# Attention within hash buckets and a mixture-of-experts stage: divisions moved to another engine, one comparison for six, and a new instruction order

## The chip, the cores and the metric

The kernel runs on one core of a Trainium2 chip. The metric is the device time of one execution in microseconds (us); three runs of the kernel before gave 447.36 us as their median (446.34 to 448.22). One further execution was taken with the hardware profiler, and all rows below are from it. A core has a matrix engine (TensorE, "PE" in the profile, its weight loads "PEld"), a vector engine (VectorE, "DVE"), a scalar engine (ScalarE, "ACT"), GpSimd ("POOL") and SyncE ("SP"), which here only issues DMAs.

## The reference

```python
# B, H, S, D = 4, 8, 768, 64; proj has 6 columns
q_bits = (einsum('bhsd,dk->bhsk', q, proj) > 0); k_bits likewise
mask   = bucket(q_bits)[..., :, None] == bucket(k_bits)[..., None, :]
scores = where(mask, q @ k.T / sqrt(D), -1e9)
attn   = exp(scores - scores.max(-1))
attn   = attn / (attn.sum(-1) + 1e-9)
x      = (attn @ v), heads side by side              # (4, 768, 512)
gate   = x @ w_gate                                  # (4, 768)
for b in range(4):                                   # the 128 tokens with the highest gate
    top = argpartition(-gate[b], 128)[:128]
    ye  = relu(x[b, top] @ w1) @ w2                  # 512 -> 1024 -> 512
    out[b, top] = x[b, top] + sigmoid(gate[b, top]) * ye   # other tokens: out = x
```

## The kernel before

There are 32 heads (head 8b+h belongs to batch b). For each head the kernel loads q and k transposed, hashes them (a matmul and a comparison, `signs`), and places the sign bits beside the head's rows as extra rows of one operand, so that one matmul gives scores with the bucket mask already in them. Three stages follow, each cut in units that the order names by short words:

- The row maxima. `mx` units (PE, L559) form bounds from the keys in two halves; `kd`, the difference of the halves, is computed once per head on DVE (L553) or POOL (L550). `re` (ACT, L567) takes the positive part, `rd` (DVE, L575) reduces it with the second matmul to a maximum per row. When all six `rd` of a head are done, `mt` (PE, L584) turns the column of maxima into a row, `mc2` (ACT, L589) copies it out of PSUM and a DMA places it as a further row of the operand.
- The scores. `s` units (PE, L604 and L608, a high and a low part) write PSUM and `e` (ACT, L622 and L624) takes the exponentials P.
- The product with V. P is split in a high half, which is read in place, and the rest R = P - high(P), which is a subtraction on DVE (`r`, L643) or on POOL (`g`, L646). `a` (PE, L668) multiplies both by V into one PSUM tile per head, with the row sums in an extra column. `rc` (DVE, L678 to L680) takes the reciprocals of the sums and `n` (ACT, L692) divides. That PSUM tile has one buffer: the next head's `a.x.0` starts when the divisions of this head are done. Input for the splits comes from `xh` (ACT, L440) and `xl` (DVE, L445), the high and low part of q and k.

After the last head of a batch, `sc` (DVE, L706) forms the gate scores and `choose` (in the order `c0`, `c1`, `c2`; for the last batch `rank_last`) ranks the tokens, marks in `sel` which token goes to which of 128 slots (L799, L1108), turns this by matmuls into indices, and gathers the tokens by an indirect DMA. `e0` to `e3` are the experts: the gathered tokens are transposed by PE (L836) and split by ACT, DVE, ACT (L843, L844, L845: xth, xtl, xtb) before the matmuls with w1 and w2. The experts of batches 0 to 2 run beside the attention of later batches.

Nothing reorders instructions at run time: each engine executes its own in the order in which the code issues them, and semaphores between engines are added where data need them. That order is a hand-written string, `ORDER`, of some 2770 words such as `mx.13.1.0` or `n.0.2`; a second string, `BANKS`, gives the PSUM bank of each `mx` tile. A POOL subtraction is issued so that it waits for the last DVE instruction issued before it that is marked with `mine` (`turn`). A `wu.N` word is filler: N matmuls of constants (L305) whose result nobody reads, put where PE would stand idle at the start.

Of the kernel before, what the change touches and what calls it, by code (L numbers as in the profile page):

```python
# [41 lines left out]
i0 wu.30 ia.0 ia.2 X.0 dd.0.3 wu.23 hx.0.1 X.1 X.2 da.0.0 sx.0.1.0 sx.0.1.1 hx.0.0 sx.0.0.1 da.0.2 sx.0.0.0  # L42
kv.0 X.3 V.0 xh.1 pa.1.0 lc pa.1.1 wu.5 h.0.0.1.2 sg.0.0.1.2 ia.1 h.0.1.1.2 sg.0.1.1.2 ps.1.1 da.0.1 wu.18
mx.0.1.0 ps.1.0 w pb.0.1 mx.0.2.0 xh.0 re.0.1 xl.0 pb.0.2 mx.0.0.0 pb.0.3 re.0.0 wu.2 mx.0.2.1 mx.0.0.1 rd.0.0
mx.0.1.1 rd.0.1 re.0.2 rd.0.2 mx.0.3.0 re.0.3 ia.3 h.0.1.2.4 sg.0.1.2.4 wu.1 mx.0.3.1 mx.0.4.0 re.0.4 ir.1
h.0.0.2.4 rd.0.3 pb.0.0 sg.0.0.2.4 ps.2.1 ir.0 wu.1 mx.0.5.0 vh.0 re.0.5 mx.0.5.1 mx.0.4.1 rd.0.4 rd.0.5
ps.2.0 kd.1 wu.16 mx.1.1.0 mx.1.0.0 xh.2 re.1.1 pa.2.1 mx.1.2.0 re.1.2 mx.1.5.0 re.1.0 vl.0 w wu.2 mx.1.0.1 mc
rt.0 rk.0 mx.1.1.1 pa.2.0 pb.1.0 rd.1.0 mx.1.3.0 rd.1.1 wu.3 mx.1.2.1 rd.1.2 wu.3 mx.1.4.0 re.1.5 re.1.3 wu.3
mx.1.5.1 mx.1.3.1 re.1.4 mx.1.4.1 w xl.1 sv.0 rd.1.3 w s.0.6 pb.1.2 xh.3 s.0.3 s.0.8 rd.1.4 w pb.1.1 e.0.6
s.0.0 e.0.3 s.0.5 e.0.8 ps.3.0 e.0.0 rd.1.5 mt.1 g.0.4 pb.1.3 mc2.1 mr.1 sh.0 pa.3.1 xl.3 s.0.4 kv.2 s.0.2  # L50
mx.2.1.0 mx.2.2.0 sl.0 ps.3.1 e.0.5 e.0.2 re.2.1 mx.2.0.1 V.1 s.0.1 mx.2.0.0 s.0.7 re.2.0 e.0.1 g.0.1 mx.2.2.1
r.0.0 a.0.0 re.2.2 e.0.7 r.0.2 rd.2.0 mx.2.1.1 rd.2.1 rd.2.2 s.1.6 X.6 e.0.4 r.0.3 mx.2.4.1 mx.2.5.0 re.2.5
xl.2 s.1.0 mx.2.3.0 e.1.0 re.2.3 mx.2.4.0 re.2.4 mx.2.3.1 rd.2.3 s.1.3 s.1.2 e.1.2 X.4 rd.2.4 g.0.5 pa.3.0
vh.1 a.0.1 a.0.2 X.5 xh.4 X.7 w e.1.3 a.0.3 pb.2.0 a.0.4 a.0.5 mx.2.5.1 e.1.6 s.1.8 e.1.8 kv.3 mx.3.0.0
mx.3.2.0 re.3.2 r.1.0 mx.3.0.1 rd.2.5 mt.2 s.1.5 e.1.5 mc2.2 re.3.0 g.1.2 rc.0 mr.2 s.1.7 e.1.7 g.1.5 s.1.1
pb.2.1 e.1.1 mx.3.1.0 n.0.0 n.0.1 r.1.4 n.0.2 pb.2.3 vl.1 rd.3.0 h.1.0.0.4 pb.2.2 sg.1.0.0.4 h.1.1.0.4
sg.1.1.0.4 s.1.4 w ps.5.0 mx.3.1.1 ps.4.1 r.1.1 re.3.1 mx.3.2.1 pa.4.0 w w mx.3.4.0 re.3.4 a.1.0 a.1.1 w a.1.2
xh.6 mx.3.5.1 mx.3.3.0 rd.3.1 rd.3.2 e.1.4 r.1.3 mx.3.5.0 re.3.3 re.3.5 pa.4.1 pb.3.2 mx.3.4.1 s.2.0 ps.4.0
xl.4 pb.3.1 s.2.1 mx.3.3.1 e.2.0 e.2.1 s.2.2 rd.3.3 rd.3.4 rd.3.5 w pb.3.3 s.2.5 s.2.3 e.2.2 xh.5 a.1.3 e.2.3
a.1.4 e.2.5 sv.1 sh.1 kd.4 mx.4.0.0 a.1.5 sl.1 re.4.0 mt.3 pa.5.1 mc2.3 mr.3 mx.4.1.0 mx.4.0.1 s.2.4 re.4.1  # L60
pa.5.0 rc.1 n.1.1 ps.5.1 n.1.0 pb.3.0 g.2.0 n.1.2 rd.4.0 mx.4.1.1 V.2 e.2.4 rd.4.1 g.2.1 mx.4.3.0 mx.4.2.0
re.4.2 re.4.3 mx.4.4.1 s.2.6 e.2.6 s.2.8 e.2.8 g.2.2 mx.4.2.1 rd.4.2 a.2.0 s.2.7 mx.4.5.0 ps.6.0 re.4.5 pa.6.1
w g.2.3 xl.5 pb.4.3 mx.4.4.0 a.2.1 pb.4.0 pb.4.2 e.2.7 a.2.2 a.2.3 kv.5 pb.4.1 mx.4.3.1 w w rd.4.3 re.4.4
s.3.3 e.3.3 s.3.4 e.3.4 s.3.5 mx.4.5.1 mx.5.2.0 e.3.5 re.5.2 s.3.0 e.3.0 rd.4.4 rd.4.5 s.3.2 w mt.4 mc2.4
mx.5.0.0 e.3.2 mx.5.1.0 mr.4 re.5.1 re.5.0 s.3.6 e.3.6 mx.5.0.1 X.8 pa.6.0 ps.6.1 mx.5.2.1 r.2.4 a.2.4 g.3.2
g.3.3 r.2.5 a.2.5 rc.2 s.3.7 X.9 vh.2 e.3.7 s.3.1 rd.5.0 e.3.1 s.3.8 e.3.8 mx.5.1.1 mx.5.4.0 mx.5.3.0 s.4.1
pb.5.2 s.4.3 n.2.1 pb.5.3 r.3.0 pb.5.0 g.3.1 rd.5.1 rd.5.2 w r.3.4 pb.5.1 n.2.2 s.4.0 mx.5.3.1 n.2.0 vl.2
mx.5.5.0 a.3.0 a.3.1 a.3.2 re.5.4 re.5.5 e.4.0 e.4.1 kv.6 g.3.5 sv.2 re.5.3 rd.5.3 mx.5.4.1 s.4.2 e.4.3 xh.7
mx.5.5.1 mx.6.5.0 re.6.5 rd.5.4 rd.5.5 xl.7 e.4.2 g.4.1 g.4.0 s.4.4 e.4.4 mx.6.1.0 s.4.5 re.6.1 mt.5 mc2.5
mx.6.0.0 mr.5 e.4.5 s.4.6 xl.6 sh.2 sl.2 V.3 re.6.0 pa.7.1 a.3.3 a.3.4 a.3.5 rc.3 e.4.6 mx.6.2.0 mx.6.0.1  # L70
n.3.1 ps.7.0 X.10 s.4.8 e.4.8 mx.6.1.1 s.4.7 g.4.4 pb.6.3 ps.7.1 rd.6.0 n.3.0 mx.6.2.1 mx.6.3.0 r.4.2 r.4.3
X.11 s.5.0 pb.6.0 rd.6.1 n.3.2 e.4.7 r.4.5 w pa.7.0 re.6.3 w w xh.8 e.5.0 pb.6.1 w s.5.2 re.6.2 a.4.0 a.4.1
a.4.2 a.4.3 a.4.4 a.4.5 rc.4 vh.3 rd.6.2 mx.6.3.1 e.5.2 n.4.0 s.5.6 e.5.6 mx.6.4.1 w g.5.0 s.5.1 mx.6.4.0
re.6.4 rd.6.3 rd.6.4 mx.6.5.1 rd.6.5 s.5.3 h.2.0.0.4 h.2.1.0.4 n.4.2 pb.6.2 e.5.1 s.5.5 mt.6 e.5.3 sg.2.0.0.4
s.5.4 n.4.1 mc2.6 mr.6 pa.8.0 kd.7 mx.7.1.0 s.5.7 e.5.5 s.5.8 mx.7.1.1 vl.3 pb.7.0 e.5.4 e.5.7 mx.7.0.0 e.5.8
r.5.1 re.7.0 g.5.2 a.5.0 pa.8.1 sg.2.1.0.4 a.5.1 a.5.2 r.5.5 ps.8.1 g.5.4 re.7.1 V.4 w w xh.9 mx.7.2.1
# [1103 lines left out]
```

## Time and profile before

| | |
|---|---|
| median of 3 runs (lowest to highest) | 447.36 us (446.34 to 448.22) |
| the profiled execution, its own time | 448.66 us |
| its span, first to last instruction | 446.8 us |
| PE busy | 430.0 us, 96% |
| DVE, ACT, POOL busy | 351.3, 343.5, 219.9 us |
| mean granted TensorE clock | 0.991 of full speed |

The profiled execution takes 1.86 us more than its span, and 1.30 us more than the median of the runs. Busy shares are means over a span whose stages have different limits. PE's own busy time contains its stretches at a lower clock and its overlap of one matmul with the next, so that 96% is no statement that PE runs at its peak. Durations of single instructions are in ns in groups by line and in us in a timeline.

### The profile page before, as it was taken

What the parts mean: (1) busy time and instruction counts of PE and PEld (TensorE: products, weight loads), DVE (VectorE), ACT (ScalarE), POOL (GpSimd) and SP (SyncE); (2) the same over time, 40 slices, a digit from 0 to 9 for tenths busy, and PEclk for the clock granted to TensorE, in tenths of its full rate; (3) what the DMA queues carried; (4) which work ended last, traced back from release to release, by engine and by line L of the source; (5) the groups of instructions that cost most, each with busy time, mean ns of one, the idle gap of its engine ahead of it and who ended that gap; (6) DMA issues with size and microseconds to landing.
All of it is one profiled execution on the core that took longest, in us unless ns stands there. A gap on an engine that the chain in (4) does not pass through costs nothing.

```text
span 446.8 us, 14202 instructions
## 1 busy us (share of the span) xinstructions
PE 430.0 (96%) x5530; PEld 353.0 (79%) x5539; DVE 351.3 (79%) x872; ACT 343.5 (77%) x830; POOL 219.9 (49%) x165
## 2 busy tenths in 40 slices
...
GB/s 253 175 216 201 216 227 222 194 218 180 246 204 181 154 158 221 111 226 198 196 161 154 168 177 194 177 177 193 206 150 155 88 143 56 37 107 25 72 49 23
DMA packets 32802, 72.72 MB, mean 163 GB/s; under 512 B 5024, under 2 KB 11372, under 8 KB 32736
## 3 DMA queue, kind: packets, MB, share of 16 engines
...
## 4 chain that ended last, share of the span: by engine, by line
PE 74%; DVE 9%; DMA 8%; issue 4%; ACT 3%; SPq 1%; POOLq 0%; ACTq 0%; POOL 0%; DVEq 0%
PE av L668 19%; PE mx L559 15%; PE st L604 13%; PE st L608 12%; DMA X<-in_qk_dram 4%; PE mh L868 4%; PE yp L906 3%; PE hp L364 3%; DVE R L643 3%; PE ws L305 2%; DMA A<-mr 2%; DVE me L575 1%; DVE jks L706 1%; DMA A<-XH 1%; PE sp L509 1%
## 5 line engine op out<-in xcount | busy, mean ns | idle before, releaser
L646 POOL TENSOR_TENSOR R<-P 128x768 f16<-128x768 f32 x100 | 158.8, 1598 | 115.8 <-ACT P L624 26.4
L604 PE MATMUL st<-A 97*128 97x512 f32 (+1 forms) x384 | 129.3, 350 | 0.4 <-DMA A<-mr 0.4
L608 PE MATMUL st<-B 128*128 128x512 f32 (+1 forms) x384 | 125.0, 340 | 0.0
L622 ACT ACTIVATE P<-st 128x512 f32<-128x512 f32 x192 | 111.9, 604 | 13.2 <-PE st L608 11.9
L575 DVE CUSTOM_DVE_ANT_0 me<-mx,me 128x384 f32<-128x384 f32 x192 | 100.8, 551 | 21.5 <-PE mx L559 11.1
L668 PEld LDWEIGHTS <-P 128*128 128x128 bf16 x2304 | 110.6, 97 | 8.3 <-issue 4.0
L668 PE MATMUL av<-V,P 128*128 128x65 f16 (+1 forms) x2304 | 116.4, 194 | 0.0
L668 PE MATMUL av<-V,R 128*128 128x65 f16 x1152 | 113.4, 192 | 1.6 <-DVE R L643 1.4
L668 PEld LDWEIGHTS <-R 128*128 128x128 f16 x1152 | 106.3, 99 | 2.3 <-DVE R L643 1.9
L567 ACT ACTIVATE me<-mx 128x384 f32<-128x384 f32 x192 | 91.6, 497 | 18.6 <-PE mx L559 14.6
L643 DVE TENSOR_TENSOR R<-P 128x768 f16<-128x768 f32 x92 | 97.1, 1079 | 8.6 <-ACT P L624 5.6
L604 PEld LDWEIGHTS st<-A 97*128 97x128 f32 x384 | 72.9, 190 | 11.1 <-issue 1.2
L608 PEld LDWEIGHTS st<-B 128*128 128x128 f32 x384 | 73.2, 190 | 3.4
L559 PE MATMUL mx<-A 96*128 96x384 f32 x192 | 64.2, 358 | 1.7 <-DVE m L575 1.5
L559 PE MATMUL mx<-kd,A 96*128 96x384 f32 x192 | 63.7, 363 | 1.4 <-DMA A<-XH 1.0
L624 ACT ACTIVATE P<-st 128x512 f32<-128x512 f32 x96 | 57.9, 603 | 3.3 <-PE st L608 3.2
L692 ACT ACTIVATE x<-av,rc 128x64 f32<-128x64 f32 x192 | 45.3, 317 | 10.4 <-DVE rc L680 9.2
L550 POOL TENSOR_TENSOR kd<-A 96x384 fp32r<-96x384 f32 x20 | 22.7, 1135 | 43.7 <-PE mx L559 29.2
L559 PEld LDWEIGHTS mx<-kd,A 96*128 96x128 f32 x192 | 35.1, 190 | 11.0 <-DVE m L575 1.9
L559 PEld LDWEIGHTS mx<-A 96*128 96x128 f32 x192 | 36.0, 191 | 8.5 <-DVE m L575 2.1
L445 DVE SCALAR_TENSOR_TENSOR XL<-X,XH 128x768 fp32r<-128x768 f32 x32 | 36.3, 1136 | 4.1 <-ACT XH L440 3.2
L440 ACT ACTIVATE XH<-X 128x768 fp32r<-128x768 f32 x32 | 27.2, 849 | 1.1 <-DVE kd L553 1.0
...
## 6 DMA issues: line engine op xcount, KB each, us to landing
...
```

Source lines behind the costliest of these rows:

```text
L445: mine(nc.vector.scalar_tensor_tensor(xl, st["X", h], XS, st["XH", h].bitcast(F32), op0=ALU.mult, op1=ALU.subtract))
L559: nc.tensor.matmul(pt[:, :384], a[0:96, 0, t * P : (t + 1) * P], a[0:96, 1, 384:768] if i else st["kd", h], start=True, stop=True,)
L567: nc.scalar.activation(me, st["mx", h, t, 0][:, :384], AF.Relu)
L575: nc.vector.tensor_tensor_reduce(out=me, in0=st["mx", h, t, 1][:, :384], in1=me, op0=ALU.add, op1=ALU.max, scale=1.0, scalar=-0.25, accum_ ...
L604: nc.tensor.matmul(pt[:, o : o + n], a[:, 1, c * P : (c + 1) * P], a[:, 0, q0 : q0 + n], start=True, stop=False,)
L608: nc.tensor.matmul(pt[:, o : o + n], bt[:, 1, c * P : (c + 1) * P], bt[:, 0, q0 : q0 + n], start=False, stop=True,)
L622: nc.scalar.activation(pp[:, r, 0:512], pt, AF.Exp, scale=ES)
L624: nc.scalar.activation(pp[:, :, 512:768], pt.rearrange("p (a b) -> p a b", a=2), AF.Exp, scale=ES)
L643: mine(nc.vector.tensor_tensor(**rest(h, c)))
L646: turn(nc.gpsimd.tensor_tensor(**rest(h, c)))
L668: nc.tensor.matmul(o[:, t, 0:n], l, vv[:, c, hh, v0 : v0 + n], start=False, stop=last and l is lo, skip_group_check=True,)
L692: nc.scalar.activation(x[:, t], o[:, t, 0:D], AF.Copy, scale=rc[:, t : t + 1])
```

## The change

The divisions. Before, each `n` word issued two ACT instructions (one per 128 query rows, 128x64 elements). After, 33 of the 96 words still do; the other 63 are `nd` words, each of which is one DVE multiplication for both (128x2x64) from PSUM by the reciprocals. The selection: six comparisons of 128x128 become one of 128x768, in `choose` for batches 0 to 2 and in `rank_last`, where the six had stood between the six matmuls that use them; each of `c0` to `c2` has one word less. The filler: 107 matmuls become 81; of these the ones ahead of the first hash go from 53 to 48, those from the first hash to the first `mx` from 23 to 19, and those behind it from 31 to 14. The rests: 83 on DVE and 109 on POOL, where 92 and 100 stood. `kd` keeps its 20 on POOL and 12 on DVE, but others of the heads. All of the order is new.

```diff
-        for t in range(2 * j, 2 * j + 2):
+        return st["x", b][:, :, hh * D : (hh + 1) * D], st["O", h], st["rc", h], slice(2 * j, 2 * j + 2)
+
+    def norm_act(h, j):
+        x, o, rc, ts = norm(h, j)
+        for t in range(ts.start, ts.stop):
             nc.scalar.activation(x[:, t], o[:, t, 0:D], AF.Copy, scale=rc[:, t : t + 1])
+
+    def norm_dve(h, j):
+        x, o, rc, ts = norm(h, j)
+        nc.vector.tensor_tensor(
+            x[:, ts], o[:, ts, 0:D], rc[:, ts].unsqueeze(2).broadcast_to([P, 2, D]), op=ALU.mult
+        )
...
+    def select(rank, sel):
+        mine(nc.vector.tensor_tensor(
+            sel, iota16.unsqueeze(1).broadcast_to([P, NC, P]),
+            rank.unsqueeze(2).broadcast_to([P, NC, P]), op=ALU.is_equal,
+        ))
...
-        for t in range(NC):
-            nc.vector.tensor_scalar(sel[:, t], iota16, rank[:, t : t + 1], None, op0=ALU.is_equal)
-            if t % 3 == 2:
-                yield
+        select(rank, sel)
+        yield
...
+        select(rank, sel)
         for t in range(NC):
-            nc.vector.tensor_scalar(sel[:, t], iota16, rank[:, t : t + 1], None, op0=ALU.is_equal)
             nc.tensor.matmul(
```

Three places of the new order matter below. The names are those of the tiles with a running number; the first tile of a row is what it writes.

The first place is the start, on ACT's queue, which issues some of the loads itself (X is q and k of a head, V the values of a pair of heads, A the operand with head 0's rows scaled). Before:

```order
L350 DMA X0_136<-in_qk_dram 64x768
L350 DMA X1_167<-in_qk_dram 64x768
L415 ACT_TABLE_LOAD
L415 ACTIVATE A0_82<-X0_136 32x768 x2
L357 DMA V0_185<-in_v_dram 128x768
L440 ACTIVATE XH1_187<-X1_167 128x768
L415 ACTIVATE A0_82<-X0_136 32x768
L716 DMA W0_234<-in_w1_dram 128x1024
L440 ACTIVATE XH0_239<-X0_136 128x768
L567 ACTIVATE me0_1_241<-mx0_1_0_231 128x384
```

After:

```order
L357 DMA V0_132<-in_v_dram 128x768
L350 DMA X0_138<-in_qk_dram 64x768
L350 DMA X1_172<-in_qk_dram 64x768
L415 ACT_TABLE_LOAD
L415 ACTIVATE A0_82<-X0_138 32x768 x2
L724 DMA W0_191<-in_w1_dram 128x1024
L415 ACTIVATE A0_82<-X0_138 32x768
L440 ACTIVATE XH1_194<-X1_172 128x768
L488 ACTIVATE V0_88<-V0_132 128x12x64
L567 ACTIVATE me0_0_225<-mx0_0_0_223 128x384
```

The load of V is now issued ahead of the two loads of X, and a copy of V stands where the second high part stood.

The second place is on DVE around the last maxima of head 13 (m13), where expert 0 begins (ye0 with ss0, xtl0). Before:

```order
L575 ISA me13_2_3524,m13_3504<-mx13_2_1_3517,me13_2_3524 128x384
L575 ISA m13_3504 128x1
L852 ISA ye0_3561,ss0_3560<-xe0_3374,wgt_72 128x512
L852 ISA ss0_3560 128x1
L445 SCALAR_TENSOR_TENSOR XL13_3583<-X13_2615,XH13_2961 128x768
L575 ISA me13_3_3553,m13_3504<-mx13_3_1_3570,me13_3_3553 128x384
L575 ISA m13_3504 128x1
L575 ISA me13_4_3547,m13_3504<-mx13_4_1_3572,me13_4_3547 128x384
L575 ISA m13_3504 128x1
L575 ISA me13_5_3549,m13_3504<-mx13_5_1_3586,me13_5_3549 128x384
L575 ISA m13_3504 128x1
L844 TENSOR_TENSOR xtl0_3628<-xp0_3555,xth0_3627 128x512
```

After:

```order
L575 ISA me13_3_3423,m13_3384<-mx13_3_1_3409,me13_3_3423 128x384
L575 ISA m13_3384 128x1
L643 TENSOR_TENSOR R11_2_3430<-P11_2_3265 128x768
L864 ISA ye0_3526,ss0_3525<-xe0_3203,wgt_72 128x512
L864 ISA ss0_3525 128x1
L575 ISA me13_4_3471,m13_3384<-mx13_4_1_3455,me13_4_3471 128x384
L575 ISA m13_3384 128x1
L575 ISA me13_5_3495,m13_3384<-mx13_5_1_3418,me13_5_3495 128x384
L575 ISA m13_3384 128x1
L856 TENSOR_TENSOR xtl0_3532<-xp0_3520,xth0_3531 128x512
```

The low part of head 13 (XL13) no longer stands between the maxima of head 13; a rest of head 11 and the same instruction of expert 0 do.

The third place is the end of the attention, head 31, with expert 2 (xth2, xtl2, xtb2) beside it. On ACT before:

```order
L622 ACTIVATE P31_1_8703<-st31_4_8709 128x512
L843 CAST xth2_8721<-xp2_8716 128x512
L845 CAST xtb2_8723<-xp2_8716 128x512
L622 ACTIVATE P31_2_8777<-st31_6_8733 128x512
L624 ACTIVATE P31_2_8777<-st31_8_8728 128x2x256
L622 ACTIVATE P31_2_8777<-st31_7_8736 128x512
```

On ACT after:

```order
L622 ACTIVATE P31_1_8562<-st31_4_8575 128x512
L622 ACTIVATE P31_2_8618<-st31_6_8602 128x512
L624 ACTIVATE P31_2_8618<-st31_8_8597 128x2x256
L622 ACTIVATE P31_2_8618<-st31_7_8592 128x512
L855 CAST xth2_8630<-xp2_8625 128x512
L857 CAST xtb2_8632<-xp2_8625 128x512
```

The two casts of expert 2 have moved from ahead of the last three exponentials to behind them. On DVE at the same place before:

```order
L643 TENSOR_TENSOR R31_1_8713<-P31_1_8703 128x768 x2
L844 TENSOR_TENSOR xtl2_8722<-xp2_8716,xth2_8721 128x512
L643 TENSOR_TENSOR R31_2_8798<-P31_2_8777 128x768 x2
L852 ISA ye2_8857,ss2_8856<-xe2_7921,wgt_72 128x512
L852 ISA ss2_8856 128x1
L678 TENSOR_SCALAR rc31_8865<-av31_8739 128x6
```

On DVE after:

```order
L643 TENSOR_TENSOR R31_2_8622<-P31_2_8618 128x768 x2
L856 TENSOR_TENSOR xtl2_8631<-xp2_8625,xth2_8630 128x512
L714 ISA jks3_1_4_8637,sc3_1_8581<-x3_7035,wgt_72,sc3_0_7972 128x192
L714 ISA sc3_1_8581 128x1
L714 ISA jks3_1_5_8639,sc3_1_8581<-x3_7035,wgt_72,sc3_0_7972 128x192
L714 ISA sc3_1_8581 128x1
L678 TENSOR_SCALAR rc31_8751<-av31_8641 128x6
```

Between the last rests and the reciprocal (rc31) now stand expert 2's low part and two passes of the gate scores.

## Rows read from the trace of the kernel before

**Rows 1.** Busy time (share of the span) and instructions of each engine
```profile
PE 430.0 (96%) x5530; PEld 353.0 (79%) x5539; DVE 351.3 (79%) x872; ACT 343.5 (77%) x830; POOL 219.9 (49%) x165
```
**Rows 2.** The chain that ended last, share of the span by engine
```profile
PE 74%; DVE 9%; DMA 8%; issue 4%; ACT 3%; SPq 1%; POOLq 0%; ACTq 0%; POOL 0%; DVEq 0%
```
**Rows 3.** Windows: us; PE, PEld, DVE, ACT, POOL busy (x); PE clock; DMA share; GB/s
```profile
0.00:10.00 10.00, 9.00 (x83) 6.71 (x84) 6.41 (x12) 5.49 (x6) 9.07 (x17) 1.00 0.81 252
20.00:150.00 130.00, 127.06 (x1706) 104.42 (x1707) 112.63 (x262) 113.78 (x275) 74.60 (x50) 1.00 0.77 210
165.00:175.00 10.00, 8.25 (x34) 5.96 (x32) 7.73 (x23) 7.22 (x19) 4.26 (x4) 0.83 0.63 177
175.00:400.00 225.00, 220.71 (x3084) 188.03 (x3087) 180.08 (x464) 179.88 (x447) 112.50 (x77) 1.00 0.57 154
415.00:422.00 7.00, 6.24 (x53) 3.86 (x52) 5.13 (x17) 1.93 (x4) 0.00 (x0) 0.76 0.15 49
```
**Rows 4.** Groups by line: count | busy us, mean ns | idle before and its releasers
```profile
L692 ACT ACTIVATE x<-av,rc 128x64 f32<-128x64 f32 x192 | 45.3, 317 | 10.4 <-DVE rc L680 9.2 <-DVE xw L1076 1.0
...
L679 DVE TENSOR_TENSOR rc<-av,rc 128x6 f32<-128x6 f32 x32 | 5.3, 166 | 1.1
...
L1076 DVE TENSOR_TENSOR xw<-av,wgt 128x384 f32<-128x384 f32 x1 | 0.5, 518 | 0.0
...
L643 DVE TENSOR_TENSOR R<-P 128x768 f16<-128x768 f32 x92 | 97.1, 1079 | 8.6 <-ACT P L624 5.6 <-ACT P L622 2.0 <-ACT me L567 0.6
...
L646 POOL TENSOR_TENSOR R<-P 128x768 f16<-128x768 f32 x100 | 158.8, 1598 | 115.8 <-ACT P L624 26.4 <-DVE R L643 24.1 <-ACT P L622 18.0
...
L799 DVE TENSOR_SCALAR sel<-iota,rank 128x128 f16<-128x128 f16 x18 | 5.5, 365 | 0.1
...
L706 DVE CUSTOM_DVE_ANT_0 jks<-x,wgt,sc 128x192 bf16<-128x192 f32 x6 | 2.2, 416 | 0.5 <-ACT x L692 0.3
...
L550 POOL TENSOR_TENSOR kd<-A 96x384 fp32r<-96x384 f32 x20 | 22.7, 1135 | 43.7 <-PE mx L559 29.2 <-DVE XL L445 4.5 <-DMA A<-XH 4.3
```
**Rows 5.** Three DVE lines: duration ns min/median/max, first and last start
```profile
L643 DVE TENSOR_TENSOR R<-P x92: 916/951/3192, 25.4 to 408.5; 128x768 f16<-128x768 f32 x92
...
L445 DVE SCALAR_TENSOR_TENSOR XL<-X,XH x32: 944/953/3184, 10.8 to 378.5; 128x768 fp32r<-128x768 f32 x32
...
L575 DVE CUSTOM_DVE_ANT_0 me<-mx,me x192: 516/552/559, 11.8 to 390.9; 128x384 f32<-128x384 f32 x192
```
**Rows 6.** Timeline of the start: start us, us, engine, line, instruction [idle before <-releaser]
```profile
4.68 0.84 ACT L415 ACTIVATE A<-X 32x768 fp32r<-32x768 f32 x1 [1.43 <-DMA X<-in_qk_dram]
...
6.94 2.17 DVE L401 TENSOR_SCALAR A<-hp 6x384 fp32r<-6x384 f32 x4 [1.92 <-PE hp L389]
...
9.14 0.56 DVE L553 TENSOR_TENSOR kd<-A 96x384 fp32r<-96x384 f32 x1
...
9.26 1.18 PE L305 MATMUL ws<-ones 128*128 128x128 f16 x18
...
10.71 1.25 ACT L567 ACTIVATE me<-mx 128x384 f32<-128x384 f32 x3 [1.65 <-PE mx L559]
```
**Rows 7.** Timeline around 165 us
```profile
162.53 3.18 DVE L445 SCALAR_TENSOR_TENSOR XL<-X,XH 128x768 fp32r<-128x768 f32 x1
...
167.20 0.23 PE L584 MATMUL mt<-identr,m 128*6 128x128 f32 x1 [1.56 <-DVE m L575]
```
**Rows 8.** Timeline of the end of the attention
```profile
405.27 0.69 DVE L844 TENSOR_TENSOR xtl<-xp,xth 128x512 fp32r<-128x512 f32 x1
...
406.00 0.58 ACT L845 CAST xtb<-xp 128x512 bf16<-128x512 f32 x1 [1.64 <-DVE xtl L844]
...
407.60 1.83 DVE L643 TENSOR_TENSOR R<-P 128x768 f16<-128x768 f32 x2 [1.64 <-ACT P L624]
...
408.62 0.20 PE L668 MATMUL av<-V,R 128*128 128x65 f16 x1 [1.09 <-DVE R L643]
...
410.19 0.16 DVE L678 TENSOR_SCALAR rc<-av 128x6 f32<-128x6 f32 x1 [0.15 <-PE av L668]
```

360 lines of the change are left out of this document (179 added, 181 removed), and 10 rows, old and new, of the table BANKS.

## The prediction

> **What bounds the kernel now.** I read the busy line first. PE is busy 430.0 of 446.8 us; DVE 351.3 and ACT 343.5 are well below it [rows 1]. The chain that ended last agrees: 74% of it is PE, DVE has 9%, ACT 3% [rows 2], which of 446.8 us are 40.2 us (DVE) and 13.4 us (ACT). Then I read the windows: in 20 to 150 us PE works 127.06 of 130, in 175 to 400 us 220.71 of 225 [rows 3], so in the long middle PE stands still only 2.94 and 4.29 us, 7.2 together. Two short windows are different: 165 to 175 us with PE 8.25 of 10 and a clock of 0.83, and 415 to 422 us with 6.24 of 7 and a clock of 0.76 [rows 3]. With the two levels 2.4 and 1.2 GHz, 0.83 over 10 us and 0.76 over 7 us each mean about 3.4 us at the lower one, which loses about 1.7 us of work per place. Before the first of them, PE had waited 1.56 us for the maxima [rows 7]. So a unit less of DVE or ACT work is worth little as such; what counts is where PE waits: at the start, at 165 us and at the end of the attention.
>
> **The divisions.** 63 words go from ACT to DVE: 126 ACT instructions less, at 45.3 us / 192 = 0.236 us of engine time each [rows 4], is -29.7 us of ACT. On DVE come 63 multiplications of 128x128 elements from PSUM with the reciprocals. No row shows this one. The nearest below is the 6-element operation on the same PSUM tile, 0.166 us, the nearest above the 384-element multiplication with a PSUM operand, 0.518 us [rows 4]; going straight from one to the other by elements gives 0.28 at 128, and I take that, as both rows are the same kind of instruction. So DVE +17.6 us (10.5 to 32.6). Nine rests go from DVE, 9 x 1.079 = -9.7 us, to POOL, 9 x 1.598 = +14.4 us [rows 4]; POOL is then at 234 us, about half the span, and PE's only visible waits for a rest are for one of DVE's [rows 8]. The selection: 18 comparisons of 5.5 us [rows 4] become three with 768 elements per partition, which I price at a DVE rest without a stall, 0.951 us [rows 5]: -2.7 us. Together DVE +5.2 us (-1.9 to +20.2), ACT -29.7.
>
> What of it lies on the path? By the chain's shares, ACT gives back 29.7 / 343.5 of its 13.4 us, -1.2 us, and DVE takes 5.2 / 351.3 of its 40.2 us, +0.6 us: -0.6 us. The ends: all of ACT's idle before the divisions that waited for the reciprocals, 9.2 us in 5 places [rows 4], cannot be worth more to PE than some 2.5 us, a third of PE's 7.2 us idle; and all of DVE's +5.2 on the path would be +5.2. A division on DVE follows its reciprocal on the same engine, with no hand-over to ACT, which is good for the one product tile that the next head waits for; but behind it on DVE the maxima and the next rests are queued, and for the maxima PE waits. The shares are a mean over both, so I stay at -0.6.
>
> The Trainium skill has a rule that speaks against the nine rests. The rows first: a DVE rest takes 951 ns as its median and up to 3192, the low parts 953 and up to 3184, and the maxima, which read one operand from PSUM, never more than 559 [rows 5]. In "SBUF — State Buffer", section "Who interferes with whom", the skill says that a DVE instruction with two SBUF inputs and a GpSimd instruction that reads SBUF exclude each other for the whole of the one that began first, and that one with at most one SBUF input is not touched. The trace agrees in its spread. By the rule nine more POOL rests can each hold a DVE instruction by up to 3.192 - 0.951 = 2.24 us, 20 us at worst, and the new divisions, which read PSUM, by nothing. By the rows the mean excess of a DVE rest over its median is 0.13 us, so that nine more cost DVE about a tenth more of 92 x 0.13 = 12 us, and I leave it in the bounds.
>
> **The filler.** Seventeen matmuls fewer behind the first maxima; 18 took 1.18 us, 0.066 each [rows 6], so 1.1 us of PE in order. There PE waits at times for data anyway, so I count half: -0.55 us (-1.1 to 0). The five fewer ahead of the first hash and the four fewer behind it stand where PE waits for X or signs: 0.
>
> **The start.** V's 384 KB are now issued ahead of the two X loads on ACT's queue. In the first 10 us the core moves 252 GB/s [rows 3]; 384 KB (393 kB) at that rate are 1.56 us by which X can land later than the 4.68 us at which ACT now begins with it [rows 6]. The signs (2.17 us, four instructions [rows 6]) then begin up to 1.56 later than 6.94. Against it, the difference of the keys needs only two of the four signs, -1.08 us; but it goes from DVE (0.56 us) to POOL (1.135 us as the mean [rows 4, 6]), +0.57. Net +1.05 us if the delay is whole, -0.5 if there is none. ACT has two instructions, a high part and a copy, ahead of the first positive part (10.71 us [rows 6]), which begins with the first product. I take 0 (-0.6 to +1.5), since V must be loaded in either order and its bytes then no longer compete with those behind it.
>
> **The stop at 165 us.** Before, the low part of head 13 stood between the maxima of that head and took 3.18 us [rows 7] in place of 953 ns [rows 5]; the three maxima behind it, and with them the turning matmul on PE, came late. In the new order that instruction is no longer there, and PE has product and maximum units ahead of the turning matmul. What can go is 1.56 us of waiting and 1.7 us of lost clock: 3.3. What is late next is expert 0, whose split by DVE and ACT still follows the maxima, and the rest of head 11 now between them, which is as open to a stretch as the low part was. I take -2.0 (-3.3 to 0).
>
> **The end of the attention.** ACT stands 1.64 us before a cast of expert 2 (0.58 us) with three exponentials behind it; DVE then waits 1.64 for P, and PE 1.09 for the rest [rows 8]. With the casts behind the exponentials these come some 2 us earlier, and one of six rests goes to POOL. But between the last rest and the reciprocal at 410.19 us now stand the low part of expert 2, 0.69 us [rows 8], and two score passes, each 0.42 [rows 4] and about 0.08 for reading its sum: 1.7 us, of which some 0.8 lie beside the products that PE makes after the last rest (409.43 us by its row [rows 8]; the reciprocal comes 0.76 us later). So 2.0 - 0.9 = -1.1 us (-2.0 to +0.5). The single comparison ahead of the last batch's index matmuls: -0.1 us. The lower clock at 418 us I leave as it is.
>
> **The sum.** On the profiled execution's own time, 448.66 us: -0.55 + 0 - 2.0 - 0.6 - 1.1 - 0.1 = -4.35, 444.3 us. That execution stands 1.30 us above the median of the runs, so the forecast is 443.0 us.
>
> **Rivals.** 1: A larger gain, 437.0 us. The stop at 165 us goes whole (3.3), the clock holds at 418 us too (1.7), the end gives 1.1 and the filler 0.55 and the selection 0.1, and with ACT 29.7 us emptier half of the middle's 7.2 us of idle goes (3.6): 10.35 less, 438.3 and 437.0 by the median. For it speaks that ACT's divisions wait 9.2 us for the reciprocals and stand ahead of exponentials; against it that PE is 98% busy there already.
> 2: Nothing to measure, 446.3 us. All the order is new, so each removed wait can be replaced: the stretched instruction of 3.18 us is one of several, and where it falls decides which wait it makes. Only the filler's 1.1 us remains: 448.66 - 1.1 - 1.30. For it speaks that rests up to 3.19 us occur on DVE and that POOL has nine more of the partners that they meet; against it that the stop at 165 us is a single large one in 225 us.
> 3: Slower, 452.6 us: VectorE becomes the bound. In 20 to 150 us DVE works 112.63 of 130 and ACT 113.78 [rows 3]; the change relieves ACT and loads DVE. If in those stretches each division holds up the maxima behind it, all of the net +5.2 us lies on the path and the waits return in other places: 448.66 + 5.2 - 1.30. This decides from the point where DVE is more than about 95% busy over a head, or where a division sits ahead of a maximum that PE waits for. For it speaks that all DVE's visible waits are short (its idle in the middle is 13%), against it that those 5.2 us are 1.2% of the span and the price can be as low as -1.9.
>
> **How the numbers follow.** Forecast 0.48 (its own range 440 to 445), larger gain 0.14, nothing 0.22, slower 0.16. What a measurement of this kernel can tell from no change is 0.5%, 2.2 us: faster is below 445.1, slower above 449.6. So faster 0.62, same 0.22, slower 0.16. The range goes from the larger gain, 436.5, to 450.0, between nothing and the slower case, with about 0.07 left out below and 0.12 above.
>
> **What would show it.** In the changed profile: DVE's multiplications at 0.2 to 0.4 us each and ACT's busy time near 314 us, DVE's near 356, POOL's near 234; no wait of over 1 us of PE for the maxima of head 13 and no lower clock near 165 us; exponentials of head 31 without expert 2's casts before them, and the last reciprocal about 1 us earlier relative to the last product; the first positive part within 1 us of 10.71. The forecast is wrong if waits of PE for DVE in the middle grow by more than 2 us, if the start is more than 1.5 us late, or if the multiplication costs over 0.5 us.

## The result: 0.75% slower

The changed kernel takes 451.55 us as the median of 15 executions against 448.90 us for the kernel before on the same chip; the ratio is 1.0075, 95% interval 1.0046 to 1.0105 (that of the two medians is 1.0059). Here and below, executions more than 1.5% above the fastest of their kernel are left out of the ratios and clocks. Forecast were 443.0 us, with a range up to 450.0. The profiled execution of the changed kernel took 453.8 us.

The busy times of the changed kernel's profile (span 451.1 us, answering to [rows 1]), and its chain by engine (to [rows 2]):

```profile
PE 423.6 (94%) x5503; PEld 349.8 (78%) x5513; DVE 348.9 (77%) x906; ACT 320.5 (71%) x704; POOL 237.7 (53%) x174
...
PE 49%; DVE 18%; DMA 13%; issue 8%; ACT 5%; POOL 4%; SPq 2%; ACTq 0%; POOLq 0%; DVEq 0%
```

PE is busy 6.4 us less than before and the span is 4.3 us longer: PE waits more, and the chain runs through DVE, DMA and POOL for shares that were PE's. The windows, in the columns of [rows 3], show where:

```profile
0.00:10.00 10.00, 7.78 (x65) 5.83 (x65) 5.15 (x9) 4.85 (x6) 8.38 (x18) 1.00 0.80 238
20.00:150.00 130.00, 122.54 (x1689) 102.67 (x1687) 108.48 (x274) 105.98 (x237) 79.33 (x54) 1.00 0.77 204
165.00:175.00 10.00, 9.92 (x122) 7.73 (x122) 7.99 (x23) 8.30 (x22) 5.23 (x4) 1.00 0.64 155
175.00:400.00 225.00, 216.04 (x2986) 183.33 (x2989) 177.97 (x475) 166.49 (x372) 125.81 (x83) 1.00 0.60 159
415.00:422.00 7.00, 5.36 (x43) 4.05 (x43) 5.19 (x18) 3.62 (x10) 0.00 (x0) 1.00 0.33 112
```

Of the places that the forecast counted on, the one at 165 us is better: PE now works 9.92 of 10 us and the clock stays at 2.4 GHz, as it does at 418 us. (These rows compare one execution of each kernel. The changed one's has a mean granted clock of 1.000, the highest of its 15, which go down to 0.987; that of the kernel before has 0.991.) But in the two long stretches PE's idle time went from 2.94 to 7.46 us and from 4.29 to 8.96 us, 9.2 us together. PE's largest waits in the changed kernel (sum, times, longest):

```profile
PE av L668 <- POOL R L646: 2.5, 4, 1.3
PE hp L364 <- DMA X<-in_qk_dram: 2.2, 2, 1.2
PE st L604 <- DMA A<-mr: 2.2, 3, 1.1
PE mx L559 <- DVE m L575: 1.9, 2, 1.6
PE st L604 <- DMA X<-in_qk_dram: 1.7, 1, 1.7
```

And in the kernel before:

```profile
PE mx L559 <- DVE m L575: 1.7, 3, 1.0
PE mt L584 <- DVE m L575: 1.6, 1, 1.6
PE av L668 <- DVE R L643: 1.4, 2, 1.1
...
PE st L604 <- DMA A<-mr: 0.4, 2, 0.2
```

Before, PE waited for none of POOL's rests, and 0.4 us in all for rows of maxima (`mr`). I added up PE's waits of 0.2 us and more in 20 to 400 us by what ended them: POOL's rests from 0 to 2.5 us, DMAs from 2.2 to 5.1, DVE from 5.2 to 6.9, ACT from 1.0 to 1.7. None of them is for a division. The instructions that the change touches, to [rows 4]:

```profile
L698 DVE TENSOR_TENSOR x<-av,rc 128x128 f32<-128x128 f32 x63 | 16.1, 286 | 6.9 <-ACT x L694 6.3
...
L694 ACT ACTIVATE x<-av,rc 128x64 f32<-128x64 f32 x66 | 16.5, 316 | 12.7 <-PE st L608 4.7 <-DVE x L698 2.9 <-PE mx L559 1.6
...
L770 DVE TENSOR_TENSOR sel<-iota,rank 128x768 f16<-128x768 f16 x4 | 3.8, 958 | 0.1
...
L643 DVE TENSOR_TENSOR R<-P 128x768 f16<-128x768 f32 x83 | 86.5, 1062 | 6.7 <-ACT P L624 4.1 <-ACT P L622 1.0 <-POOL R L646 0.6
...
L646 POOL TENSOR_TENSOR R<-P 128x768 f16<-128x768 f32 x109 | 174.1, 1608 | 146.8 <-DVE R L643 39.5 <-DVE kd L553 16.5 <-PE mx L559 13.6
```

The prices were right: 0.286 us for a multiplication (forecast 0.28) and 0.958 for the single comparison (0.951). What no row of before could show stands in the idle columns: DVE's multiplications wait 6.3 us for ACT's divisions, and ACT's wait 2.9 us for DVE's. In 23 of the 32 heads both engines divide.

### The profile page after: what moved, and what is told of

It reads as the page before. It is cut to its first block, busy times and chain, and to the rows that moved or that the text cites. A ratio compares the mean times of both kernels' runs of the same rounds, so it can differ in the third digit from the quotient of the medians.

```text
span 451.1 us, 14060 instructions
## 1 busy us (share of the span) xinstructions
PE 423.6 (94%) x5503; PEld 349.8 (78%) x5513; DVE 348.9 (77%) x906; ACT 320.5 (71%) x704; POOL 237.7 (53%) x174
## 4 chain that ended last, share of the span: by engine, by line
PE 49%; DVE 18%; DMA 13%; issue 8%; ACT 5%; POOL 4%; SPq 2%; ACTq 0%; POOLq 0%; DVEq 0%
PE av L668 13%; PE mx L559 10%; PE st L604 9%; PE st L608 8%; DVE R L643 4%; DMA X<-in_qk_dram 4%; PE yp L918 3%; DMA A<-mr 3%; DVE me L575 3%; POOL R L646 2%; PE mh L880 2%; DMA A<-XH 2%; DVE cm L755 2%; DVE cm L757 1%; DVE jks L714 1%
## 5 line engine op out<-in xcount | busy, mean ns | idle before, releaser
L646 POOL TENSOR_TENSOR R<-P 128x768 f16<-128x768 f32 x109 | 174.1, 1608 | 146.8 <-DVE R L643 39.5
L604 PE MATMUL st<-A 97*128 97x256 f32 (+1 forms) x384 | 128.6, 348 | 4.7 <-DMA A<-mr 2.2
L608 PE MATMUL st<-B 128*128 128x256 f32 (+1 forms) x384 | 125.1, 340 | 0.0
L643 DVE TENSOR_TENSOR R<-P 128x768 f16<-128x768 f32 x83 | 86.5, 1062 | 6.7 <-ACT P L624 4.1
L559 PE MATMUL mx<-A 96*128 96x384 f32 x192 | 62.7, 355 | 1.4 <-ACT me L567 0.7
L445 DVE SCALAR_TENSOR_TENSOR XL<-X,XH 128x768 fp32r<-128x768 f32 x32 | 32.7, 1026 | 0.4 <-DMA B<-XL 0.2
L694 ACT ACTIVATE x<-av,rc 128x64 f32<-128x64 f32 x66 | 16.5, 316 | 12.7 <-PE st L608 4.7
```

Of the source, the lines that this page charges most:

```text
L445: mine(nc.vector.scalar_tensor_tensor(xl, st["X", h], XS, st["XH", h].bitcast(F32), op0=ALU.mult, op1=ALU.subtract))
L559: nc.tensor.matmul(pt[:, :384], a[0:96, 0, t * P : (t + 1) * P], a[0:96, 1, 384:768] if i else st["kd", h], start=True, stop=True,)
L604: nc.tensor.matmul(pt[:, o : o + n], a[:, 1, c * P : (c + 1) * P], a[:, 0, q0 : q0 + n], start=True, stop=False,)
L608: nc.tensor.matmul(pt[:, o : o + n], bt[:, 1, c * P : (c + 1) * P], bt[:, 0, q0 : q0 + n], start=False, stop=True,)
L643: mine(nc.vector.tensor_tensor(**rest(h, c)))
L646: turn(nc.gpsimd.tensor_tensor(**rest(h, c)))
```

## The experiments

All ratios are to the kernel before on the same chip, with 95% intervals. The mean granted clock is over the executions of a kernel; "at full clock" is the median of time x clock in us, an estimate of the time without the stretches at 1.2 GHz. The kernel before (107 executions) has 0.9934 and 445.3 by it, the changed one 0.9949 and 449.2.

| kernel | order | ratio | clock | at full clock |
|---|---|---|---|---|
| e11 selection alone | before | 0.9935 (0.9902 to 0.9967) | 0.9954 | 443.0 |
| e12 filler alone | before | 1.0022 (0.9989 to 1.0056) | 0.9918 | 445.4 |
| e7 selection, filler | before | 0.9933 (0.9906 to 0.9960) | 0.9952 | 443.5 |
| e8 two words moved | before | 1.0037 (1.0007 to 1.0066) | 0.9923 | 446.8 |
| e1 division alone | before | 1.0313 (1.0252 to 1.0374) | 0.9825 | 455.4 |
| e3 all three edits | before | 1.0339 (1.0269 to 1.0409) | 0.9828 | 455.9 |
| e6 division, whole heads | before | 1.0204 (1.0160 to 1.0248) | 0.9852 | 450.9 |
| e9 e7 + whole heads behind rc | before | 0.9972 (0.9943 to 1.0000) | 0.9939 | 444.8 |
| e10 as e9, 11 heads | before | 1.0050 (1.0020 to 1.0080) | 0.9915 | 445.9 |
| e17 as e9, mixed heads | before | 1.0283 (1.0241 to 1.0326) | 0.9864 | 454.5 |
| e2 division undone | after | 1.0664 (1.0612 to 1.0716) | 0.9770 | 468.1 |
| e13 six comparisons again | after | 1.0179 (1.0151 to 1.0208) | 0.9892 | 451.9 |
| e14 nine rests back on DVE | after | 1.0232 (1.0195 to 1.0269) | 0.9882 | 453.8 |
| e15 no mixed heads | after | 1.0027 (1.0003 to 1.0051) | 0.9957 | 448.3 |
| e4 loads behind rows | after | 1.0012 (0.9977 to 1.0048) | 0.9959 | 448.0 |
| e5 e4 + start | after | 1.0047 (1.0019 to 1.0076) | 0.9933 | 447.5 |
| e16 e4 + e15 | after | 1.0081 (1.0054 to 1.0109) | 0.9910 | 448.4 |

**The edits of the code in the old order.** e1 changes only the words, in place:

```diff
-n.1.1 ps.5.1 n.1.0 pb.3.0 g.2.0 n.1.2
+nd.1.1 ps.5.1 nd.1.0 pb.3.0 g.2.0 nd.1.2
...
-n.4.2
+nd.4.2
```

> The order, the selection and the filler of the kernel before; only the 63 divisions that the change moved are single VectorE multiplications. Theory (the new order lost the time, in waits that stood nowhere before): the divisions alone are worth what ScalarE's and VectorE's shares of the chain gave, -2.5 to +1 us, ratio to the kernel before 0.994 to 1.002, and the multiplication costs 0.29 us here too. Rival (VectorE became the bound): 63 x 0.286 = 18.0 us of VectorE are not paid for by fewer rests here, and if a third or more of that lies on the path the kernel is slower by 4 to 8 us, ratio 1.009 to 1.018.

Measured 1.0313: neither 0.994 to 1.002 nor within the rival's 1.018. ACT stood 17.3 us before divisions, for DVE's. The profile of e1 at PE's longest wait for a division (timeline; ACT's exponentials are queued behind, and head 10's first product matmul waits):

```profile
145.65 0.28 DVE L686 TENSOR_TENSOR x<-av,rc 128x128 f32<-128x128 f32 x1
...
149.50 0.28 DVE L686 TENSOR_TENSOR x<-av,rc 128x128 f32<-128x128 f32 x1
149.81 0.32 ACT L682 ACTIVATE x<-av,rc 128x64 f32<-128x64 f32 x1 [3.96 <-DVE x L686]
...
150.38 0.49 PE L643 MATMUL av<-W,zs 128*128 128x396 f16 x1 [2.62 <-ACT x L682]
```

DVE's two words stand 3.85 us apart in its queue, and ACT's third begins only when the second is done, although the three write different parts of x. So a head in which both divide waits for the later engine, and ACT with it.

e3 adds the selection and the filler to e1 (the diffs shown ahead of the prediction, with filler words 30, 18, 5, 14, 2, 1, 1, 1, 2, 3, 3, 1):

> The three edits of the code in the order of the kernel before: 63 divisions on VectorE, the selection in one comparison, and 81 matmuls of filler (48 ahead of the first hash, 19 up to the first product, 14 behind it). Theory: at least as fast as the kernel before, ratio 0.992 to 1.000 (-0.6 for the divisions, -0.55 for the filler, -0.3 for the selection). Rival (one of the three edits costs the time): ratio 1.004 or more.

Measured 1.0339, as the rival has it: one of the three edits costs the time, and the other two do not make up for it. e7 is e3 without the division, e11 and e12 take its two parts alone (the filler words, without what stands between them):

```diff
-wu.30 wu.23 wu.5 wu.18 wu.2 wu.1 wu.1 wu.16 wu.2 wu.3 wu.3 wu.3
+wu.30 wu.18 wu.5 wu.14 wu.2 wu.1 wu.1 wu.1 wu.2 wu.3 wu.3 wu.1
```

> The kernel before in its own order with only the selection in one comparison and the 81 matmuls of filler, all divisions on ScalarE. Theory: -0.5 to -1 us, ratio 0.996 to 1.001. Rival (the filler that is left out had kept TensorE at its higher clock or covered a wait): ratio 1.003 to 1.01, with a lower granted clock in the first 40 us.

> The kernel before with the selection in one comparison and nothing else (107 matmuls of filler). Theory (the 3 us of e7 are the selection's: a wait near 257 us in batch 1's choice and the stretch at the lower clock near 418 us): ratio 0.992 to 0.997. Rival (the filler): 0.999 to 1.001.

> The kernel before with 81 matmuls of filler and nothing else. Theory (the selection is what gained in e7): ratio 0.998 to 1.002. Rival (the filler): 0.993 to 0.997.

e7's 0.9933 is a larger gain than its theory had, e11's 0.9935 is the selection's alone, as its theory had it, and e12's 1.0022 says that the filler is worth nothing that can be measured. The selection by itself beats both kernels. Where it gains: of the kernel before, the first choice's comparisons on DVE, the POOL rest beside them, and PE at the same place,

```profile
146.63 1.79 DVE L799 TENSOR_SCALAR sel<-iota,rank 128x128 f16<-128x128 f16 x3
...
146.69 1.52 POOL L646 TENSOR_TENSOR R<-P 128x768 f16<-128x768 f32 x1 [2.50 <-DVE rank L796]
...
148.95 0.44 PE L559 MATMUL mx<-A 96*128 96x384 f32 x1 [1.00 <-DVE m L575]
```

and of e11:

```profile
147.38 0.96 DVE L757 TENSOR_TENSOR sel<-iota,rank 128x768 f16<-128x768 f16 x1
...
148.51 1.47 POOL L633 TENSOR_TENSOR R<-P 128x768 f16<-128x768 f32 x1 [3.57 <-DVE sel L757]
148.87 0.44 PE L546 MATMUL mx<-A 96*128 96x384 f32 x1 [0.17 <-DVE m L562]
```

Before, the POOL rest began beside the first of three small comparisons, and one of them took as long as it. The times of all 18, shortest, median and longest in ns:

```profile
L799 DVE TENSOR_SCALAR sel<-iota,rank x18: 242/247/1459, 146.6 to 357.1; 128x128 f16<-128x128 f16 x18
```

In e11 the POOL rest waits for the end of the single comparison. That wait is written into the code: `select` marks its comparison with `mine`, which the six were not, and POOL's rest waits for the last marked instruction (`turn`). So e11 changes two things, one instruction for six and the mark, and which of them gains was not tested. PE's wait for the maxima behind falls from 1.00 to 0.17 us. Behind this place, the steps by which the profile of e11 gains on that of the kernel before are 0.3 us near 180 us, two of 0.5 us around the second choice (at 262 us), and the stretch at the lower clock near 418 us, which is gone in this execution.

e6, e9, e10 and e17 ask what in the division costs. e6 is e1 with 21 whole heads on DVE; e9 and e10 have whole heads (21, 11) directly behind the reciprocal, with e7's selection and filler; e17 has the change's own mixed words there (the diff is of e17):

```diff
-rc.1 n.1.1 ps.5.1 n.1.0 pb.3.0 g.2.0 n.1.2
+rc.1 nd.1.0 nd.1.1 nd.1.2 ps.5.1 pb.3.0 g.2.0
...
-rc.4 vh.3 ... n.4.0 ... n.4.2 ... n.4.1
+rc.4 nd.4.2 n.4.0 n.4.1 vh.3
```

> The order of the kernel before with 63 divisions on VectorE, as in e1_division_alone, but 21 heads go over whole and 11 stay whole on ScalarE, so that no head has both. In e1 the divisions of one head on two engines waited for each other: ScalarE stood 17.3 us and VectorE 6.6 us before a division of a mixed head, with exponentials and rests queued behind. Theory (that hand-over inside a head is the larger part of the 14 us): ScalarE's idle time before its divisions falls from 17.3 to some 5 us, and the ratio to the kernel before is 1.003 to 1.015. Rival (VectorE is late at the places where the words of the old order stand, mixed or not): the product's first matmul still waits 5 us and more for divisions, ratio 1.020 to 1.035.

> e7_select_filler (ratio 0.9933) with the 21 whole heads of e6_whole_heads on VectorE, the three multiplications of a head standing directly behind its reciprocal. Theory (VectorE was late at the places where the division's words stand in the old order, which were set by ScalarE's queue): TensorE's waits for divisions ahead of a head's first product matmul go from 4.3 us to under 1, ratio 0.990 to 1.000. Rival (the work itself, 0.86 us per head in VectorE's queue ahead of the maxima and rests that TensorE waits for): the waits for maxima and rests grow in their place, ratio 1.005 to 1.015.

> The same with 11 heads (every third) on VectorE in place of 21. Theory of the place: as e9_behind_reciprocal, ratio 0.990 to 0.998. Rival (VectorE's work): the cost goes with the number of heads, half of what e9 loses against 0.9933.

> e9_behind_reciprocal (old order, selection and filler of the change, ratio 0.9972) with the change's own 63 words on VectorE and 33 on ScalarE, all directly behind the reciprocal, VectorE's first: 21 whole heads against as many words in mixed heads. Theory (mixing costs by itself, about 0.5% as in e15): ratio 1.001 to 1.006, ScalarE idle before its divisions for VectorE's. Rival (directly behind the reciprocal the hand-over is short, and mixing costs only where the words stand apart): 0.995 to 0.999.

e6's 1.0204 lies at the rival's edge: with the words in the old places, mixing is a third of e1's loss (1.1%), and the rest is the place of the words and the work itself. e9's 0.9972 bears out the place: moved directly behind the reciprocal, the same heads cost 0.4% against e7, where they cost 2.0% in e6. e10 fits neither theory: with half the heads its interval lies above e9's, and why is open. e17's 1.0283 is against both of its theories: mixed heads directly behind the reciprocal cost 3.1% against e9, six times what the theory had. ACT's divisions in the lists by line (idle time before them and what ended it), first of e17, then of e9:

```profile
L682 ACT ACTIVATE x<-av,rc 128x64 f32<-128x64 f32 x66 | 16.3, 313 | 23.9 <-DVE x L686 21.2 <-PE st L596 2.5 <-DVE rc L668 0.2
```

```profile
L682 ACT ACTIVATE x<-av,rc 128x64 f32<-128x64 f32 x66 | 15.7, 320 | 2.9 <-DVE rc L668 1.8 <-DVE xw L1076 1.0
```

As many ACT divisions: 21.2 us of waiting for DVE's divisions against none. PE feels it through the exponentials that are queued behind ACT's divisions, for which it waits 3.7 us in e17 and 0.3 in e9:

```profile
PE st L592 <- ACT P L610: 3.7, 4, 2.0
```

e17 differs from e9 in a second thing: its ACT words stand directly behind the reciprocal, where e9 has its whole ACT heads in their old places. So the 3.1% are mixing together with that place; a wait for the reciprocal itself is only 0.2 us of e17's row.

**The two words.** e8 moves, in the kernel before, what the forecast wanted gone at 165 us and at 408 us (`pb.13.2`, a copy of the low part into the operand, goes with `xl.13`):

```diff
-xl.13 pb.13.2 mx.13.5.1 a.11.4 a.11.5 rd.13.3 rd.13.4 rd.13.5 e0 s.12.3 mt.13 vh.7 g.12.1 rc.11 mc2.13 e0 pb.13.3
+mx.13.5.1 a.11.4 a.11.5 rd.13.3 rd.13.4 rd.13.5 e0 s.12.3 mt.13 vh.7 g.12.1 rc.11 xl.13 mc2.13 e0 pb.13.2 pb.13.3
...
-r.31.3 e2 s.31.8 s.31.6 s.31.7 a.31.0 a.31.1 e.31.6 e.31.8 a.31.2 r.31.4 e.31.7 a.31.3 a.31.4 r.31.5 a.31.5
+r.31.3 s.31.8 s.31.6 s.31.7 a.31.0 a.31.1 e.31.6 e.31.8 a.31.2 r.31.4 e.31.7 a.31.3 a.31.4 r.31.5 e2 a.31.5
```

> The kernel before with two words moved: the low part of head 13 behind the last maxima of that head and the reciprocal of head 11, and expert 2's transposes and split behind the last rest of head 31. Theory (the stops at 165 us and 408 us are what these two words make): the wait of 1.56 us and the 3.4 us at the lower clock near 165 us go, the last reciprocal comes 1 to 2 us earlier, ratio to the kernel before 0.991 to 0.996. Rival (the waits move on to the next instruction in the queue): 0.997 to 1.002.

Measured 1.0037, slightly above both ranges. PE's largest waits in e8:

```profile
PE st L591 <- DMA A<-mr: 4.2, 3, 3.5
PE mx L546 <- POOL kd L537: 2.1, 1, 2.1
```

The wait for the maxima of head 13 is gone, and head 13's scores wait 3.5 us for the row of them instead (at 176.9 us). The same exponentials of both kernels, the kernel before first, tell what each move was worth in this one execution (454.8 us, 4 us above the kernel's median):

```profile
163.83 0.60 ACT L624 ACTIVATE P<-st 128x512 f32<-128x512 f32 x1 [0.24 <-PE st L608]
170.80 1.04 ACT L622 ACTIVATE P<-st 128x512 f32<-128x512 f32 x2
180.56 0.60 ACT L622 ACTIVATE P<-st 128x512 f32<-128x512 f32 x1
...
406.48 0.60 ACT L622 ACTIVATE P<-st 128x512 f32<-128x512 f32 x1
```

```profile
167.69 0.60 ACT L611 ACTIVATE P<-st 128x512 f32<-128x512 f32 x1 [0.19 <-PE st L595]
172.54 1.05 ACT L609 ACTIVATE P<-st 128x512 f32<-128x512 f32 x2
186.98 0.60 ACT L609 ACTIVATE P<-st 128x512 f32<-128x512 f32 x1
...
410.63 0.60 ACT L609 ACTIVATE P<-st 128x512 f32<-128x512 f32 x1 [0.42 <-PE st L595]
```

The execution is 3.9 us late ahead of the first moved word, 1.7 behind it, 6.4 at 187 us, and 4.2 at the last exponentials. So behind the first move 2.1 us are gained, as forecast, and by 187 us 4.7 are lost again, 3.5 of them PE's wait for the row; between there and the last exponentials, at the tail's move, 2.3 are gained. The late row is of e8's own making, as far as its queue shows: the row is ready when ACT's copy ends at 170.99 us, and SyncE issues it at 173.60, behind the copies of the moved low part and a load of X:

```profile
170.76 0.23 ACT L576 CAST mr<-mt 6x128 fp32r<-6x128 f32 x1
...
171.12 1.16 SPq L439 DMA_DIRECT2D B<-XL  x2
172.33 1.17 SPq L339 DMA_DIRECT2D X<-in_qk_dram  x1
173.60 0.73 SPq L439 DMA_DIRECT2D A<-mr  x1
```

**In the new order.** e2 puts all divisions back on ACT, e13 the six comparisons, e14 nine rests on DVE, e15 each mixed head on the engine that has two of its three (for e14 and e15 the changed words alone, e15's of the first two mixed heads):

```diff
-g.10.5 g.22.3 g.27.0 g.27.5 g.27.4 g.9.5 g.13.0 g.4.1 g.17.4
+r.10.5 r.22.3 r.27.0 r.27.5 r.27.4 r.9.5 r.13.0 r.4.1 r.17.4
...
-nd.0.0 nd.0.1 n.0.2 n.4.0 n.4.1 nd.4.2
+nd.0.0 nd.0.1 nd.0.2 n.4.0 n.4.1 n.4.2
```

> The changed kernel with all 96 divisions as pairs of ScalarE instructions again, in the new order. Theory (the new order): it stays slower than the kernel before, ratio 1.004 to 1.015, since the waits for the rows of maxima near 66 and 101 us and for the rests do not hang on the division. Rival (VectorE became the bound): without the 18 us on VectorE it is back at the kernel before or better, ratio 0.990 to 1.000.

> The changed kernel with the six comparisons in place of the one, in its own order (a second word behind that of the selection, as before). Theory (the single comparison is worth about 3 us in either order, and the new order and the division give back that and 3.4 us more): ratio to the kernel before 1.012 to 1.018, against 1.0075 for the changed kernel. Rival (the gain hung on the place at 148 us of the old order, and the new order makes nothing of it): ratio 1.005 to 1.010.

> The changed kernel with nine rests back on VectorE (92 and 100, as before), among them those for which TensorE waited 0.98, 0.37, 0.32 and 1.44 us. Theory (POOL's rests, 1.47 us long and up to 2.24, come late where they are a head's last): these waits go, ratio 1.001 to 1.005. Rival (VectorE then is late itself, with maxima behind the rests): ratio 1.006 to 1.012.

> The changed kernel with each head's divisions on the engine that has at least two of its three, in the same places of the order: 78 words on VectorE, 18 on ScalarE, none mixed. Theory (in mixed heads the engines waited for each other, 6.3 us of VectorE and 2.9 us of ScalarE, and the new order is not free of it): ratio 1.000 to 1.006. Rival (the new order was made for exactly this division and hides those waits): 1.007 to 1.015.

e2 is against both of its theories: at 1.0664 it shows that the new order suits only its own divisions. There ACT's last division of a batch comes late, the gate scores on DVE wait for it (4.43 us), and the maxima queued behind the scores keep PE for 7.2 us. e13's 1.0179 is at its theory's edge: the six comparisons cost 1.0% in the new order, where the single one gained 0.65% in the old. e14 is against its theory and beyond its rival: with nine rests (9.7 us by [rows 4]) back on DVE the time grows by 1.6%, 7 us, and the maxima are late:

```profile
PE mt L572 <- DVE m L563: 6.0, 5, 2.6
```

So in this order DVE's work lies on the path to a large part, and the move of rests to POOL was needed. e15 takes 0.5% off by unmixed heads, although DVE has 15 words more by it (78 for 63); 0.9 us of that remains at full clock.

e4 and e5 move loads, because with large loads under way a row of 3 KB came late (issued at 62.0 us, its scores at 67.6):

```diff
-X.11 s.3.6 mx.5.3.0 mt.4 re.5.1 mc2.4 mr.4
+s.3.6 mx.5.3.0 mt.4 re.5.1 mc2.4 mr.4 X.11
...
-s.6.5 V.4 pa.9.0 xh.10 mt.7 mc2.7 kd.8 mx.8.1.0 mx.8.4.0 mx.8.2.0 mr.7 e.6.5 lg
+s.6.5 pa.9.0 xh.10 mt.7 mc2.7 kd.8 mx.8.1.0 mx.8.4.0 mx.8.2.0 mr.7 V.4 X.12 e.6.5
...
-ia.0 V.0 ia.1 X.0 dd.0.3 ia.3 wu.18 hx.0.1 sx.0.1.1 hx.0.0 X.1
+ia.0 ia.1 X.0 dd.0.3 ia.3 wu.18 hx.0.1 sx.0.1.1 hx.0.0 X.1 V.0
```

> The changed kernel with four loads moved: X of head 11 behind the row of maxima of head 4, X of head 12 and V of pair 4 behind that of head 7, the gate weights further back. Theory (these rows landed 4.5 and 5.4 us after their issue because loads of 384 KB and more were under way): they land 1 to 2 us after their issue, the waits of 1.88 and 1.27 us of TensorE near 66 and 101 us go, and the kernel is 2 to 3.2 us faster than the changed one, ratio to the kernel before 1.000 to 1.003. Rival (the rows are late for another reason, or the wait only moves on): ratio stays at 1.006 to 1.009.

> The changed kernel with the loads moved as in e4_rows_first, and V of pair 0 behind both loads of X at the start, its copy on ScalarE behind the positive part of unit 4. Theory (V's 384 KB ahead of X cost the hash of head 1 some 1.1 us of waiting): the first positive part comes about 0.9 us earlier than in the changed kernel (11.61 us), ratio to the kernel before 0.996 to 1.001. Rival (what the start gains is lost again while the next loads of X land, at the hash near 38 us): the first positive part is earlier, but the ratio stays at 1.000 to 1.004 as in e4.

> e15_unmixed (ratio 1.0027) with the four loads of e4_rows_first moved as well. Theory (the hand-over in mixed heads and the rows of maxima behind large loads are two separate parts of what the new order lost): ratio 0.996 to 1.000. Rival (they are one loss, counted twice, or the loads only move the wait on): 1.001 to 1.005.

In e4 PE's waits for rows fall from 2.2 us in 3 places to 0.6 in one; the hash near 38 us waits 2.1 us for X, where it waited 1.2. The ratio, 1.0012, lies in the theory's range, and its interval ends below the rival's; the medians of all executions, 450.83 over 448.96 us, give 1.0042. In e5 the first positive part begins at 11.16 us (11.61 in the changed kernel), half of what the theory had, and the ratio, 1.0047, is no better than e4's. e16, with both corrections, is at 1.0081, where neither theory had it: unmixing gains 0.5% on the changed kernel and loses 0.7% on e4. At full clock e4, e5, e15 and e16 stand at 447.5 to 448.4 us, so by this estimate most of what separates their ratios is time at 1.2 GHz; what each correction is worth in the new order stays open.

## Why the prediction was wrong

- **The division, the step that failed.** The sum has one term for the long middle, the divisions with the rests and the comparison, costed by the engines' shares of the chain at -0.6 us; in its place PE stands 9.2 us longer in the two long stretches. The term rested on "a division on DVE follows its reciprocal on the same engine, with no hand-over to ACT". But 23 heads are mixed, and there the divisions of one engine wait for the other's, with all that is queued behind. In the old order this is shown: the divisions alone cost 3.1% (e1), unmixed heads in the same places 2.0% (e6), directly behind the reciprocal 0.4% unmixed (e9 against e7) and 3.5% mixed (e17 against e7). No arrangement that was tried gained. In the changed kernel the link is argued only in part: its order has no PE wait for a division left, DVE's divisions wait 6.3 us and ACT's 2.9, and PE's longer waits are for POOL's rests, rows and loads. That these are the price of an order made around the mixed divisions fits e2 (1.0664 without them), but no run shows it.
- **The engine sums.** The price of a multiplication was right, and ACT came near (320.5 us against 314). DVE was to be busy 5.2 us longer (-1.9 to +20.2) and is busy 2.4 us less, just outside that range.
- **The selection, mis-sized.** Counted at -2.7 us of DVE by shares, and -0.1 us at the end. Measured alone: -0.65%, 2.9 us. At 148 us the maxima were queued directly behind the comparisons, and PE waited for these: 0.83 us less on DVE (1.79 to 0.96) took 0.83 us off PE's wait, and a share of the whole chain does not see such a place.
- **The stops at 165 and 408 us.** Both went in the changed kernel as forecast, with 1.67 and 1.41 us more PE work in their windows; the second, in the kernel before and in the changed one:

```profile
400.00:415.00 15.00, 13.47 (x161) 10.70 (x162) 10.70 (x27) 8.37 (x23) 1.47 (x1) 1.00 0.25 86
```

```profile
400.00:415.00 15.00, 14.88 (x230) 12.68 (x228) 12.23 (x31) 6.11 (x13) 2.96 (x2) 1.00 0.05 20
```

  In one execution e8 bears the sizes out at each place, 2.1 and 2.3 us against the 2.0 and 1.1 counted, but in the total the two moves bring +0.4%, since its row of maxima came late behind the moved copies. So these terms fit their places, and no run shows them as a gain of the whole.
- **The filler and the start.** The filler was forecast at -0.55 us, measured at 0 within its interval. At the start the first positive part came 0.9 us later, inside the range given; the hash of head 1 waited 1 us for X behind V, and e5, with V behind X, gives half of the 0.9 us back.
- **The rivals.** The slower case, 452.6 us, is the nearest number, and by luck: it wanted 5.2 us more work on DVE, which did not come, and PE's waits for DVE in 20 to 400 us grew by 1.7 us only. What speaks for it is that the chain's DVE share went from 9% to 18%, and that e14, with nine rests back on DVE, shows the 6.0 us of late maxima that it described. "All the order is new, so each removed wait can be replaced" (the second rival) is what the changed kernel's profile shows, at a higher price: 9.2 us more idle time in the long stretches in place of the 3.3 us at 165 us.
- **The signs of being wrong.** None of the three came: the waits for DVE grew by less than 2 us, the start was 0.9 us late, the multiplication took 0.286 us. They looked at DVE and the start, and the time was lost in waits for POOL's rests, rows and loads in the middle.

By a sentence of the Trainium skill's "SBUF — State Buffer", section "Who interferes with whom", a DVE comparison with a scalar can use both port pairs and then excludes GpSimd, or is excluded by it. The trace agrees: such a comparison takes 247 ns as its median and 1459 beside the POOL rest above. The prediction, which took every instruction with one SBUF input as untouched, left this mode out. The multiplications, which read one operand from PSUM, were never held:

```profile
L698 DVE TENSOR_TENSOR x<-av,rc x63: 279/285/294, 38.1 to 417.7; 128x128 f32<-128x128 f32 x63
```

The rests behaved better than the worst case of the prediction: with nine more on POOL, DVE's mean fell from 1079 to 1062 ns. The code keeps POOL's rests behind marked DVE instructions (`turn`), so this is no test of the rule.

What stays open: the changed kernel is 1.4% behind e7. Unmixed heads (e15) and moved loads (e4) each give about half a per cent back alone and nothing together (e16); the rest lies over many waits of up to 1.7 us (late rows and loads, late rests on POOL, late maxima). Why the program makes ACT and DVE wait for each other was not tried either: their divisions of a head write different parts of x, but all read one PSUM tile, and no run separates the two.
